# A unit of seven products for query block 4 and FFN block 12, and a new order of loads and transposes at the start

## The chip, the cores and the metric

The kernel runs on one core of one Trainium2 chip. The core has TensorE (PE in the profile: matmuls, with the loading of weights shown apart as PEld), VectorE (DVE), ScalarE (ACT), GpSimd (POOL), and SyncE (SP), which here only issues DMAs. The metric is the device time of one execution in microseconds; less is better.

## What is computed

A layer norm without weights, a linear attention of 32 heads and a gated feed-forward block share one normed input; the result is added to the input. There are 2048 tokens of width 640, and the inner width of the feed-forward block is 1728. All inputs are bf16.

```python
x  = A_x                                   # (1, 2048, 640)
xn = layernorm(x, eps=1e-5)
q, k, v = split(xn @ wqkv)                 # 32 heads of 20
phi = lambda t: where(t > 0, t + 1, exp(t)) + 1e-6
kv  = einsum("bhsd,bhse->bhde", phi(k), v);  z = phi(k).sum(tokens)
o   = (phi(q) @ kv) / (phi(q) . z + 1e-6)
s   = o @ wo
g   = silu(relu(xn @ w1) @ w2)             # w1 (640, 1728), w2 (1728, 640)
out = x + s * g
```

## The kernel before

**Tiles.** The tokens are 16 tiles of 128 (t = 0 to 15) and four chunks of 512 (j = 0 to 3). The width 640 is C = 5 pieces of 128. The inner width 1728 is 13 blocks of 128 (f = 0 to 12) and a half block of 64. A block of Q or of the feed-forward block for one chunk is five matmuls of 512 columns that add up in one bank of PSUM (`Q_mm` L764, `H_mm` L801); a tile of K is ten matmuls of 320 columns in two banks (`K_mm` L708). The half block is computed for two chunks at once by matmuls with 32 columns of weights, four beside each other (`H_half` L811).

**Units of seven.** Most blocks are made by a scheme with seven products instead of eight. `unit` (L1169) takes two blocks of weights and two chunks and forms the four results from seven products of two matmuls each, plus the fifth piece of the width: 18 matmuls, where four single blocks take 20. Its steps are named s1, s5, s6, s2, s7, s3, s4. The sums and differences of operands that it needs are made by DVE beforehand: `h_T` of the tokens (`T0` for chunks 0 and 1, `T1` for 2 and 3), `h_S`, `q_S`, `k_S` and `m_S` of the weights (`SH0` to `SH2`, `SQ`, `SK`, `SM`). In a unit ACT copies two products out (L1210), DVE adds in s6 (L1223), and DVE adds once more for the last result. `a` and `b` are units of the feed-forward block for chunks 0, 1 and for 2, 3, `p` and `q` those of Q, `k` of K. `m_unit` (L1287) pairs block 4 of Q with block 12 of the feed-forward block, since each is left over: before, `m1` does this for chunks 2 and 3 alone.

**The head.** While x and the weights come in, tiles 0 to 3 are not normed, but centred (`centre`, L671, with half the mean by DVE and half by ACT, or all by ACT), transposed by TensorE against an identity (`transposes`, L684), copied out of PSUM (`xcT_copy`, L691), and multiplied with the key weights (`K_mm`) and with five blocks of w1 (`HP`, L1365: 4, 5, 10, 11, 12). The scale 1/std is applied later: to K by ACT's exponential and relu (`K_evac`, L721), to the blocks of `HP` by DVE (`scale_h`, L1093, called by `ZS`). Means and variances come from DVE (`bn`, L633, two halves of a tile, and `aggr`, L638), the power -1/2 from POOL (L643). `LN_norm` (L653) writes the normed tile and issues its transposing DMA on SP (`xnT_dma`, L702), which gives the transposed tile `xnT` from which all the rest is computed. The first 32 matmuls of TensorE (`fill`, L602) compute nothing.

**Order.** All operations are recorded with what they read and write. `Sched.place` (L189) then plans every engine with estimated durations. TensorE and SP keep the order in which their operations are recorded; ACT, DVE and POOL do so up to `end_of_head` (L186), and behind it take the most urgent of the first 60 that can run. The recorded order is written by hand in the head (L576 to L592 the loads, L835 to L889 and L1377 to L1392 the rest), and behind it is the text `PROGRAM` (L345), whose words `play` (L1569) carries out: `p0.s1` is step s1 of unit p0, `H110` is block 10 of chunk 1, `Q14` is block 4 of Q in chunk 1, `Kb8` the second half of the key tile 8, `hh0` the half block of chunks 0 and 1, `n8` norm and transpose of tile 8, `xa` and `wa` loads of x and of w1. The text begins

```text
H110 H112 H14 H111 T0 H15 SQ SK xa Q14 a0.s1 a0.s5 Q04 a0.s6 p1.s5 p1.s1 ...
```

w1 comes in seven pieces, w1[0] to w1[6] (`w1_load`, L557; piece d holds the blocks 2d and 2d + 1, the last piece block 12 and the half block), the key weights in up to five (`wk_load`, L563). SP issues the loads of the head in this order: x0, key weights 0, 1, 2, 3-4, w1[2], w1[5], x4, x5, w1[6], x6, x7, w1[0], w1[3]; ACT issues x1, x2, x3. Then SP issues the transposes of tiles 4, 5, 6, 7, the loads of x8-9 and of wq, and the transposes of 0, 1, 2, 3.

**The end.** The last tile is finished in pieces (`s_last`, L1869): columns 0 to 160 and 160 to 320 (`LC`, L1649) come from the last ten matmuls, and each is multiplied, added to x and stored.

## Time and profile before

| | |
|---|---|
| time, median of 3 runs | 202.5 us (202.43 to 202.83) |
| span of the profiled execution, first to last instruction | 201.4 us |
| TensorE busy | 197.8 us (98%) |
| DVE, ACT, POOL busy | 175.1, 130.9, 37.9 us |
| granted TensorE clock | 1.000 |
| first matmul with data | 4.50 us |
| last matmuls begin, last instruction ends | 198.17 us, 201.4 us |

For the profiled execution the profile gives the span and no other time; the median of the runs is 1.1 us above it. In the profile, L714 is the line of the K matmuls, L804 of the blocks of the feed-forward block, L766 of Q, L1203 of the units of the first half, L1030 of the units behind them, L822 of the half blocks, L687 of the transposes, L975 the helper that records most of DVE's sums. A row of the timeline gives the start, the length, the engine and the line; neighbouring instructions of one kind are merged and counted. Matmuls are pipelined: the length of a single one holds the emptying of the pipe, so that the distance of two starts is what one costs. In the table of stages, the columns are the length, then the busy time of PE, PEld, DVE, ACT, POOL with counts, the granted clock, and DMA.

### The profile page before, as it was taken

The page shows a single profiled execution, that of the slowest core. Times are in us where ns is not written, and L with a number is a line of the kernel's source. Part 1 is how long each engine was busy: PE and PEld are TensorE (multiplying, and loading weights), DVE is VectorE, ACT ScalarE, POOL GpSimd, SP SyncE. Part 2 cuts the span into 40 slices and gives each one's busy share as a digit, 9 for nine tenths or more (in the row PEclk, how much of TensorE's full clock was granted, in tenths as well). Part 3 has the DMA queues.
Part 4 walks back from the last instruction along what each step waited for, and adds up shares of the span by engine and source line. Part 5 has one row for each costly group of instructions (what it writes and reads, how often), then busy time and mean ns, then how long its engine had stood idle before and what let it go on. Part 6 is the DMA issues. An engine that isn't in the chain of part 4 may idle for free.

```text
span 201.4 us, 3693 instructions
## 1 busy us (share of the span) xinstructions
PE 197.8 (98%) x1340; PEld 122.6 (61%) x1340; DVE 175.1 (87%) x413; ACT 130.9 (65%) x273; POOL 37.9 (19%) x66
## 2 busy tenths in 40 slices
PE   8999999999999999999999999999999999999995
PEld 7655644455455454445654777777777777767773
DVE  5988999999999888999975999999779786985674
ACT  6598957998999999978653224371555555445643
POOL 3174060363134654152200000000000000000000
PEclk9999999999999999999999999999999999999999
DMA  6977974765545896575910987865961244012103
GB/s 196 326 211 120 264 174 30 189 164 119 116 92 107 163 260 131 102 142 104 245 34 2 324 217 207 263 201 145 373 232 65 68 163 165 0 67 68 65 33 98
DMA packets 38471, 30.43 MB, mean 151 GB/s; under 512 B 13749, under 2 KB 38453, under 8 KB 38453
## 3 DMA queue, kind: packets, MB, share of 16 engines
q1 hardware_dynamic: 32581, 23.28, 41.2%
q0 software_dynamic: 4624, 5.57, 14.3%
q10 hardware_dynamic: 1248, 1.35, 2.1%
q8 instruction: 10, 0.16, 0.3%
q14 instruction: 8, 0.07, 0.1%
HBM read 15.81 MB, written 5.24 MB: 105 GB/s over the span
## 4 chain that ended last, share of the span: by engine, by line
PE 95%; DMA 3%; SPq 1%; DVE 0%; issue 0%; DVEq 0%
PE psT L1030 43%; PE psT L1203 31%; PE psT L714 8%; PE psT L804 5%; DMA reg<-in_A_wqkv_dram 3%; PE psT L1501 2%; PE psT L1835 1%; PE psT L822 1%; PE psT L766 1%; PE psT L1626 1%; PE psT L1600 1%; PE psT L934 1%; DVE reg L975 0%; SPq L564 0%; SPq L540 0%
## 5 line engine op out<-in xcount | busy, mean ns | idle before, releaser
L1203 PE MATMUL psT<-reg 128*128 128x512 bf16 (+2 forms) x159 | 41.7, 370 | 0.0
L1030 PE MATMUL psT<-reg,regH 128*128 128x320 bf16 (+1 forms) x224 | 34.8, 299 | 0.0
L1030 PE MATMUL psT<-reg 128*128 128x320 bf16 (+1 forms) x178 | 29.4, 299 | 0.0
L1030 PEld LDWEIGHTS psT<-reg,regH 128*128 128x128 bf16 (+1 forms) x224 | 21.8, 98 | 8.7 <-DVE psT L975 0.2
L1203 PEld LDWEIGHTS psT<-reg 128*128 128x128 bf16 (+1 forms) x159 | 15.5, 98 | 16.1 <-DVE reg L975 0.7
L902 POOL DMA_DIRECT2D regH<-reg x16 | 18.4, 1238 | 27.0 <-DMA regH<-reg 9.4
L1037 ACT ACTIVATE reg<-psT 128x320 f32<-128x320 f32 (+1 forms) x24 | 10.4, 435 | 17.4 <-PE psT L1030 15.9
L1030 PEld LDWEIGHTS psT<-reg 128*128 128x128 f16 (+1 forms) x178 | 17.3, 98 | 7.2 <-DVE regH L1256 0.4
L975 DVE TENSOR_TENSOR reg<-reg 128x1024 f16<-128x1024 bf16 (+10 forms) x30 | 18.9, 645 | 0.7 <-PE psT L1203 0.6
L1253 ACT ACTIVATE regH<-psT 128x512 bf16<-128x512 f32 (+1 forms) x24 | 14.6, 607 | 4.1 <-PE psT L1203 3.9
L975 DVE TENSOR_TENSOR psT<-psT,reg 128x320 f32<-128x320 f32 (+1 forms) x22 | 11.9, 542 | 5.6 <-PE psT L1030 5.1
L1030 PE MATMUL psT<-reg,pqT 128*128 128x320 bf16 (+1 forms) x84 | 16.3, 299 | 0.0
L1662 ACT ACTIVATE wv_sb<-psT 128x320 bf16<-128x320 f32 (+1 forms) x22 | 9.2, 423 | 10.3 <-PE psT L1030 9.9
L635 DVE BATCH_NORM_STATS2 stats<-reg 128x6 f32<-128x320 bf16 x32 | 13.9, 475 | 1.9 <-DMA reg<-in_A_x_dram 1.9
L1850 ACT ACTIVATE reg<-psT 128x640 bf16<-128x640 f32 (+1 forms) x14 | 8.0, 570 | 9.2 <-PE psT L1030 9.2
L714 PE MATMUL psT<-reg 128*128 128x320 bf16 x80 | 12.3, 299 | 0.0
L1037 ACT ACTIVATE psT<-psT 128x320 f32<-128x320 f32 x17 | 7.3, 427 | 6.8 <-PE psT L1030 6.8
L975 DVE TENSOR_TENSOR reg<-psT,reg 128x320 f32<-128x320 f32 (+2 forms) x19 | 9.5, 504 | 1.4 <-PE psT L1030 1.3
L781 ACT ACTIVATE regE<-psT 128x512 bf16<-128x512 f32 x16 | 9.6, 607 | 1.1 <-PE psT L766 0.5
L714 PEld LDWEIGHTS psT<-reg 128*128 128x128 bf16 x80 | 7.8, 98 | 4.3 <-ACT regH L808 0.3
L643 POOL TENSOR_TENSOR rsy<-rsv,mhalf 128x1 f32<-128x1 f32 x16 | 10.0, 622 | 1.3
L1030 PEld LDWEIGHTS psT<-reg,pqT 128*128 128x128 bf16 (+1 forms) x84 | 8.2, 98 | 3.2
(170 smaller groups left out, 397.9 us busy)
## 6 DMA issues: line engine op xcount, KB each, us to landing
regH<-reg POOLq DMA_DIRECT2D x16, 320.0 KB, 3.7
reg<-in_B_w_dram SPq DMA_DIRECT2D x12, 320.0 KB, 4.6
scr<-rden SPq DMA_DIRECT2D x4, 640.0 KB, 6.7
reg<-in_A_x_dram SPq DMA_DIRECT2D x4, 640.0 KB, 6.3
out_dram<-reg SPq DMA_DIRECT2D x14, 160.0 KB, 1.8
regE<-scr SPq DMA_DIRECT2D x3, 640.0 KB, 5.3
reg<-in_A_x_dram SPq DMA_DIRECT2D x4, 320.0 KB, 3.8
reg<-in_A_wo_dram SPq DMA_DIRECT2D x6, 160.0 KB, 5.0
```

The source lines that it names most:

```text
L635: sc.op("DVE", lambda eng: eng.bn_stats(stats[:, t, a, :], xv[:, HN * a:HN * (a + 1)]), R=[("xin", xs(t))], W=[("stats", t, a)])
L643: sc.op("POOL", lambda eng: eng.tensor_tensor(out=rsy[:, t:t + 1], in0=rsv[:, t:t + 1], in1=mhalf[:, :], op=ALU.pow), R=[("rsv", t), ("mha ...
L714: fns.append(lambda eng, a=a, k=k, lhs=lhs: eng.matmul(ps[bk[a]][:, 0:HN], lhsT=lhs, rhs=wk[:, k, HN * a:HN * (a + 1)], start=(k == 0), st ...
L781: exps.append(sc.op("ACT", lambda eng: eng.activation(out=e_, in_=src, func=ACTF.Exp), R=[key], W=[("er_e", es)]))
L804: sc.group("PE", [(lambda eng, k=k: eng.matmul(ps[b], lhsT=w1_col(k, P * f, P), rhs=src[:, k, :], start=(k == 0), stop=(k == C - 1))) for ...
L902: dma("POOL", lambda eng: eng.dma_start(zacc[a], src, **kw), R=[key] + after, W=[("zacc", a)], chain=zchain[a])
L975: sc.op("DVE", lambda eng: eng.tensor_tensor(out=out, in0=in0, in1=in1, op=op), R=R, W=W, extra=extra)
L1030: sc.group("PE", [(lambda eng, k=k, lhs=lhs, rhs=rhs: eng.matmul(ps[b][:, 0:HN], lhsT=lhs, rhs=rhs, start=(start and k == 0), stop=(k == n ...
L1037: sc.op("ACT", lambda eng: eng.activation(out=dst, in_=ps[b][:, 0:HN], func=ACTF.Copy), R=[("ps", b)], W=[dkey], extra=extra)
L1203: sc.group("PE", [(lambda eng, k=k, lhs=lhs, rhs=rhs: eng.matmul(ps[b][:, 0:nn], lhsT=lhs if tile is None else rhs, rhs=rhs if tile is Non ...
L1253: sc.op("ACT", lambda eng: eng.activation(out=dst, in_=ps[b], func=ACTF.Relu), R=[("ps", b)], W=[("hT", j, f)], extra=ex)
L1662: sc.op("ACT", lambda eng, lo=lo, hi=hi: eng.activation(out=g[:, lo:hi], in_=src[:, lo - HN * n:hi - HN * n], func=ACTF.Silu), R=[key, ("s ...
```

## The change

- The blocks H012 (in `HP`), H112, Q04 and Q14 go; the unit `m0` (block 4 of Q and block 12 of the feed-forward block, chunks 0 and 1) comes, behind `p1`. `SM`, its operand sums, moves ahead of it. `ZS` scales four blocks of chunk 0 instead of five.
- The head is now part of the text, ahead of a word `|`. Its key products are cut into smaller steps (`k012`: tile 0, pieces 1 up to 2).
- Loads of the head, all on SP but x1: x0, x2, key weights 0, 1, x3, key weights 2-3 (one transfer), x5, x4, key weight 4, x7, w1[2], x6, w1[5], w1[3], w1[0]. Then the transposes of tiles 5, 4, 2, 7, 6, 3, 0, 1 in one run, then wq, w1[6], x8-9, x12-13, x10-11, w1[4], the transpose of tile 8, and so on.
- The variance of tiles 1 and 2 comes from ACT (`square`: the sum of squares of the centred tile), not from DVE's statistics; their norm uses the mean that ACT had made.
- Behind the head four key tiles (5, 4, 7, 6), H15 and H111 stand ahead of the first unit; H110 and H14 stand between steps of units. `hh0` and `hh1` are no longer neighbours.
- `LC` is 0, 192, 320. The planner's estimates of loads change, and so may the order that it gives to ACT, DVE and POOL.

```diff
@@ Sched: estimates of DMAs
-            o.byt = 0.6 if o.turn else size / {"scr": 205e3}.get(names[0], {"scr": 240e3}.get(names[1], 310e3))
+            o.byt = 0.6 if o.turn else size / {"scr": 205e3}.get(names[0], {"scr": 240e3, "in_A_x_dram": 365e3, "in_A_wqkv_dram": 365e3}.get(names[1], 300e3))
...
+        lags = [(3.8, 0.6), (13.0, 0.7)]
...
-                line = max(est + (2.0 if c.turn else 1.5), line + (0.8 if turned and not c.turn else 0.0)) + c.byt
+                line = max(est + (2.0 if c.turn else 1.5), line + (turned != c.turn) * (0.4 if c.turn else 0.8)) + c.byt
+                if lags and line > lags[0][0]:
+                    line += lags.pop(0)[1]
@@ PROGRAM
-H110 H112 H14 H111 T0 H15 SQ SK xa Q14 a0.s1 a0.s5 Q04 a0.s6 p1.s5 p1.s1 n8 wa xb a0.s2 a0.s7 p1.s6 rb a0.s3 a0.s4 p1.s3 a1.s5 a1.s1 ...
+lx0 ba0 mh0 lx2 ax1 ma0 lk01 lk12 lx3 mv6 lk24 lx5 ce0 lx4 lk45 lx7 ma1 bb0 lw2 lx6 ma2 tr0 cd0 ce1
+lw5 pf3 cd1 lw3 ce2 k001 tr1 sq1 ma3 ag0 k012 cd2 tr2 ca5 cd3 ba3 cd4 mh3 ce3 k101 lw0 k112 k123 k201
+k134 S5 tr3 S4 k024 k045 sq2 ca7 ca6 N5 S7 N4 k145 k301 k312 N2 S6 ke0 bb3 k212 k223 k324 kr0 N7
+k235 ke1 kr1 k345 ag3 SH0_1 SH0_2 N6 P4 F1 N3 ke2 N0 kr2 P10 ke3 N1 lq P11 P5 lw6 F0 lx8 kr3
+|
+xb xa KT5 S8 wb n8 wa F2 n12 n11 KT4 SM F3 SK KT7 F4 KT6 xc rb H15 n10 F7 H111 SH0_3
+a0.s1 n9 n13 H110 n14 T0 F6 n15 SQ T1 a0.s5 a0.s6 H14 p1.s1 a0.s7 a0.s2 y1 p1.s5 a0.s4 y4 SH0_4 a0.s3 p1.s6 m0.s1
+p1.s2 m0.s5 m0.s6 m0.s2 p1.s3 m0.s7 p1.s7 m0.s3 m0.s4 p1.s4 Kb8 a1.s1 Ka8 a1.s5 p0.s5 a1.s6 p0.s1 Ka12 a1.s7 p0.s6 SH1 a1.s3 a1.s2 a1.s4
+a2.s5 hh0 a2.s1 p0.s2 p0.s7 Kb12 a2.s6 F5 Ka11 ...
+y6 k1.s6 k1.s2 y12 hh1 k1.s7 b0.s7 ...
@@ head
+    BY_ACT = (1, 2)
+    def square(t):
+        junk = ek[:, eks(t), 1, :]
+        sc.op("ACT", lambda eng: eng.activation(out=junk, in_=xn[:, t, :], func=ACTF.Square, scale=D ** -0.5,
+                                                accum_out=mv[:, t, 1:2]),
+              R=[("xn", t)] + ([("xn", t, 0)] if t == 0 else []), W=[("mv", t), ("ek_r", eks(t))])
+        root(t)
...
     def LN_norm(t):
+        mean, key = (msum[:, t, 1:2], ("msum", t, 1)) if t in BY_ACT else (mv[:, t, 0:1], ("mv", t))
@@ m_unit
-                sc.op("ACT", lambda eng: eng.activation(out=hT[:, NF - 1, schunk(j)], in_=ps[b], func=ACTF.Relu),
+                sc.op("ACT", lambda eng: eng.activation(out=(hT if j else hTh)[:, NF - 1, schunk(j)], in_=ps[b],
+                                                        func=ACTF.Relu), R=[("ps", b)], W=[("hT", j, NF - 1)])
@@
-    HP = (4, 5, 10, 11, 12)
+    HP = (4, 5, 10, 11)
@@
-    LC = [0, 160, 320]
+    LC = [0, 192, 320]
```

In the new head, `lx`, `ax`, `lk`, `lw` are loads (`ax` on ACT), `ba`, `bb`, `ag` statistics on DVE, `ma` a mean on ACT, `sq` the pass of `square`, `ce` centring, `tr` transposes on TensorE, `cd` and `ca` their copies on DVE and ACT, `ke` and `kr` the exponential and relu of K, `P` a block of `HP`, `KT` a whole key tile, `S` statistics, `N` norm with transposing DMA, `F` the end of a key tile on DVE, `pf` matmuls that compute nothing.

More of the change, by code (lines that the diff above doesn't have):

```diff
@@ L347 @@
+o3.s3 u5.s4 oS5 o3.s4 e3 oS4 o4.s1 u6.s1 uSa7 o4.s5 o4.s6 u6.s5 u6.s6 o4.s7 o4.s2 o4.s3 o4.s4 u6.s7 u6.s2 o5.s1 o5.s5 u6.s4 oS6 o5.s6
+u6.s3 o5.s7 u7.s1 o5.s2 o5.s3 u7.s5 uSb7 o5.s4 u7.s2 o6.s1 o6.s5 e0 o6.s2 o6.s6 f0 u7.s6 o6.s3 o6.s7 u7.s7 o6.s4 u7.s3 e1 f3 f1
+u7.s4 l0 l1
 """
```

183 lines of the change are left out of this document (88 added, 95 removed).

## The prediction

> **What bounds the kernel now.** I read the page first, then who waited for whom, then TensorE's instructions in order of time, then the loads.
>
> ```profile
> span 201.4 us, 3693 instructions
> PE 95%; DMA 3%; SPq 1%; DVE 0%; issue 0%; DVEq 0%
> ```
>
> ```profile
> PE psT L603 <- PEq L1946: 0.8, 1, 0.8
> PE psT L714 <- DMA reg<-in_A_wqkv_dram: 0.3, 1, 0.3
> ```
>
> The chain that ended last is TensorE for 95%, and in the whole run TensorE waits visibly twice: 0.8 us before its first instruction, and once for a piece of the key weights (wqkv). Everything else is either TensorE at work or the start and the tail. The start and one stretch behind it, from the timeline of TensorE:
>
> ```profile
> 4.50 0.63 PE L687 MATMUL psT<-ident,reg 128*128 128x128 bf16 x5
> 6.70 0.44 PE L687 MATMUL psT<-ident,reg 128*128 128x128 bf16 x5
> 7.43 1.53 PE L714 MATMUL psT<-reg,regX 128*128 128x320 bf16 x10 [0.29 <-DMA reg<-in_A_wqkv_dram]
> 12.07 5.56 PE L804 MATMUL psT<-regX,reg 128*128 128x512 bf16 x25
> 17.50 5.59 PE L714 MATMUL psT<-reg 128*128 128x320 bf16 x40
> 22.93 5.56 PE L804 MATMUL psT<-reg 128*128 128x512 bf16 x25
> 28.33 1.24 PE L766 MATMUL psT<-reg 128*128 128x512 bf16 x5
> 29.41 0.59 PE L1203 MATMUL psT<-reg 128*128 128x512 bf16 x2
> ```
>
> The first column is the start. 25 matmuls of 512 columns go from 22.93 to 28.33: 5.40 us, 0.216 each, 1.08 for a block of five. 40 of 320 columns go from 17.50 to 22.93: 0.136 each, 1.36 for a key tile. The two stretches follow each other without a gap. So from 7.43 on the time is the number of matmuls, and what the change can do is take matmuls away, or put waits between them; a faster DVE or ACT in itself is worth nothing.
>
> **Part 1: the unit of seven for query block 4 and FFN block 12.** It removes the head's `H_block(0, 12)`, H112, Q04 and Q14, each five matmuls of 512 columns: 20. The unit m0 has 2+3+3+3+2+2+2+1 = 18 (the dictionary in `unit`, L1187). Two fewer at 0.216: **-0.43 us**, all on TensorE. What hides the unit's evacuations is that ACT has room and DVE is paid for below.
>
> **Part 2: the two half blocks.** Before, `hh0 hh1` stand side by side in the program; after, `hh0` stands between `a2.s5` and `a2.s1`, and `hh1` between `y12` and `k1.s7`. These are matmuls of 32 columns of weights, four at a time:
>
> ```profile
> 51.77 0.38 PE L1203 MATMUL psT<-reg 128*128 128x512 bf16 x1
> 52.07 2.34 PE L822 MATMUL psT<-reg 128*32 128x512 bf16 x40
> 54.35 0.60 PE L1203 MATMUL psT<-regE,reg 128*128 128x512 f16 x2
> ```
>
> One matmul of 512 columns stands at 51.77 and the next instruction starts at 52.07: 0.30 instead of 0.216, so 0.08 to go in. The 40 are ten rounds, 10 x 0.216 = 2.16, and take 52.07 to 54.35, 2.28: 0.12 to come out. One stay costs 0.20 us; there will be two stays instead of one: **+0.20 us**. No semaphore is involved, so nothing hides it.
>
> **Part 3: the order of the loads in the head.** Before, SP issues x0, then the key weights in pieces k0, k1, k2, k3-4; ACT issues x1, x2, x3 beside it. After, SP issues x0, x2, k0, k1, x3, k2-3 (one transfer), x5, x4, k4, x7, ...; ACT issues only x1. Issue times and the time from issue to landing (last column) of the pieces that matter:
>
> ```profile
> 0.79 0.40 SPq L540 DMA_DIRECT2D reg<-in_A_x_dram  x1
> 1.25 1.85 SPq L564 DMA_DIRECT2D reg<-in_A_wqkv_dram  x4
> ```
>
> ```profile
> reg<-in_A_x_dram SPq DMA_DIRECT2D x1, 160.0 KB, 2.5
> reg<-in_A_x_dram ACTq DMA_DIRECT2D x1, 160.0 KB, 2.7
> reg<-in_A_wqkv_dram SPq DMA_DIRECT2D x1, 160.0 KB, 5.2
> reg<-in_A_wqkv_dram SPq DMA_DIRECT2D x1, 320.0 KB, 5.7
> ```
>
> ```profile
> 2.19 5.20 DMA reg<-in_A_wqkv_dram
> ```
>
> x0 lands at 0.79 + 2.5 = 3.3. k2, the third of the four wqkv pieces, is issued at 2.19 (chain) and lands at 7.38; with x0, x1, k0, x2, k1, x3 ahead of it, it is the 7th transfer of 160 KB. k3-4, the last of the four, issued 0.45 later, lands at about 2.65 + 5.7 = 8.35, as 8th and 9th: 0.48 each. In the new order k2 comes together with k3, as 7th and 8th (x0, x1, x2, k0, k1, x3 ahead): 7.38 + 0.48 = **7.86**.
>
> TensorE's work ahead of the first use of k2 is the same in both: three transposed tiles, and four pairs for k0 and k1 (`k001 k012 k101 k112` against `K_mm(0,2,0,1)`, `K_mm(0,2,1,KA)`, `K_mm(1,4,0,KA)`: 8 matmuls). The last of it, the third transposed tile, was over at 6.70 + 0.44 = 7.14, and the wait ended at 7.43. The new DVE order puts one `bn` of tile 0 ahead of the copies of the transposed tiles:
>
> ```profile
> L635 DVE BATCH_NORM_STATS2 stats<-reg 128x6 f32<-128x320 bf16 x32 | 13.9, 475 | 1.9 <-DMA reg<-in_A_x_dram 1.9
> ```
>
> That moves TensorE by 0 to 0.475, to 7.14 to 7.62, in any case before k2-3; the wait ends at 7.86 + 0.05 = 7.91. Against 7.43 that is **+0.47 us**. Bounds: if the transfers keep the pace of the first two, whose landings are 0.79 + 2.5 = 3.3 and 0.96 + 2.7 = 3.7, k2-3 would be there at 3.3 + 7 x 0.4 = 6.1, TensorE would go on at about 7.2, and the term is -0.23; if the pair lands when k3-4 did, 8.35, it is +0.97. I take the row that has the same bytes ahead.
>
> Behind it: k4 is 11th, 7.86 + 3 x 0.48 = 9.3; `k045` comes ten matmuls and one transposed tile (at most 0.44) later, 7.91 + 10 x 0.136 + 0.3 = about 9.55. Cover 0.25; if it is gone it costs what is missing. x5 lands 9th, 7.86 + 0.48 = 8.35, and x4 near 8.8.
>
> **Part 4: the transposing DMAs in one run.** SP's issues in the old order, the group of the wq load, and what a norm waits for:
>
> ```profile
> 20.34 0.47 SPq L545 DMA_DIRECT2D reg<-in_A_wqkv_dram  x1
> ```
>
> ```profile
> L703 SPq DMA_TRANSPOSE reg<-reg x8: 1200/1299/1809, 14.1 to 25.5; - x8
> ...
> DMA to landing us min/median/max: 2.6/3.0/5.4
> ```
>
> ```profile
> reg<-in_A_wqkv_dram SPq DMA_DIRECT2D x1, 800.0 KB, 5.3
> ```
>
> ```profile
> L639 DVE BATCH_NORM_AGGREGATE mv<-stats 128x2 f32<-128x12 f32 x16 | 3.3, 204 | 0.3
> ```
>
> ```profile
> L643 POOL TENSOR_TENSOR rsy<-rsv,mhalf 128x1 f32<-128x1 f32 x16 | 10.0, 622 | 1.3
> ```
>
> SP issues one each 1.3 us. New: the first tile (5) is normed about 10.5 (x5 at 8.35, two `bn` 0.95, an aggregation 0.2, POOL's power 0.62, the rest for the hand-overs and the norm), and w1[0] is issued by then, by the pace of the old one, whose 17 loads were out by 10; SP's eight issues then take until 10.5 + 8 x 1.3 = 21 at the earliest, and the last tile lands 2.6 to 3.0 later, 23.5 to 24. Queued behind them on SP are the wq load, w1[6] and x8. Who waits: the key tiles 5, 4, 7, 6 from 12.07 + 0.48 + 4 x 1.08 = 16.9 on (tile 5 must have landed, 10.5 + 3.0: covered), and `a0.s1`, which needs all eight tiles, at 16.9 + 4 x 1.36 + 2 x 1.08 (H15, H111) = **24.5**. Covered by 0.5 to 1 us; cost 0, and if the cover is gone, what is missing. One wait is added on DVE: in the head, `SH0_1` stands ahead of the norms 6, 3, 0, 1 and needs w1[0], the last load.
>
> ```profile
> 9.07 1.04 SPq L560 DMA_DIRECT2D reg<-in_B_w_dram  x2
> ```
>
> ```profile
> reg<-in_B_w_dram SPq DMA_DIRECT2D x2, 320.0 KB, 6.0
> ```
>
> The last two of the old order were issued at 9.07 and half a microsecond later and landed 6.0 later in the median, 15.1 to 15.6. New, with less ahead, w1[0] lands at 14 to 15.6, and norm 6 comes at 15 to 16.5, where its place in SP's run is 10.5 + 4 x 1.3 = 15.7. So the cover at `a0.s1` may shrink by 0.8, to nothing in the worst of this. The old kernel first used them at 29.41, so a late tile was free there and is not here. wq (800 KB) was issued at 20.34 and landed 5.3 later; new, issued at about 21.5, it lands near 26.5, and `p1.s1` needs it at 24.5 + 2 x 0.22 + 2 x 1.08 + 4 x 0.22 = 28.0. Cover 1.5.
>
> **Part 5: variance of tiles 1 and 2 on ACT, tail.** Four `bn` and two aggregations leave DVE; ACT takes two `Square` passes of 640 columns, beside TensorE's wait for k2-3, and their results go to the norms of tiles 1 and 2, which are 3rd and 8th in the run. A pass of that width:
>
> ```profile
> 3.79 0.72 ACT L666 ACTIVATE regE<-reg 128x640 bf16<-128x640 bf16 x1
> ```
>
> Cost 0; what it costs without that cover is that ACT's copy of a transposed tile behind a pass comes 0.72 later. The last block is cut 192 + 128 instead of 160 + 160: the last product and sum on DVE are 32 columns shorter.
>
> ```profile
> 198.79 0.67 DVE L975 TENSOR_TENSOR reg<-psT,wv_sb 128x160 bf16<-128x160 f32 x2 [0.22 <-PE psT L1835]
> 199.37 0.38 DVE L975 TENSOR_TENSOR reg<-reg 128x160 bf16<-128x160 bf16 x2
> ```
>
> Two of 160 take 0.67 and 0.38, so 32 columns of one product and one sum are 0.2 x (0.33 + 0.19) = 0.10, but the piece before, which is ahead of them on DVE, grows by the same: between -0.10 and 0; I take **-0.03**, since the rows stand close behind each other.
>
> **Sum.** -0.43 + 0.20 + 0.47 - 0.03 = +0.21. The span goes from 201.4 to 201.6. The median of the runs is 202.5, 1.1 above the profiled span; I keep that distance: **202.7 us**. A difference under 0.2%, 0.4 us, can't be told from none.
>
> **Rivals.**
>
> B, the weights are not late. The wait at 7.43 was the only one behind the start; if the transfers come at the early pace, the term of part 3 is -0.23 instead of +0.47: 202.0 us. For it: the first landings are 0.4 apart. Against it: the following ones in the same trace were not.
>
> C, slower: DVE becomes the pace of the middle. It decides if DVE, and not TensorE, is late at the first operands of a unit.
>
> ```profile
> 25.00:30.00 5.00, 5.00 (x25) 2.25 (x23) 4.97 (x13) 2.78 (x5) 3.26 (x9) 1.00 0.85 182
> 40.00:60.00 20.00, 20.00 (x135) 10.08 (x134) 19.95 (x54) 19.07 (x41) 8.09 (x14) 1.00 0.55 120
> ```
>
> The first figure is the length, then come PE, its weight loads, and DVE: 4.97 of 5, 19.95 of 20. It has no room in these stretches.
>
> ```profile
> L975 DVE TENSOR_TENSOR psT<-psT,wv_sb 128x512 f32<-128x512 f32 x10 | 6.9, 694 | 1.0 <-PE psT L1203 1.0
> L975 DVE TENSOR_TENSOR regH<-psT,wv_sb 128x512 bf16<-128x512 f32 x8 | 5.5, 687 | 1.2 <-PE psT L1203 1.1
> L1266 DVE TENSOR_SCALAR regH<-regH 128x512 bf16<-128x512 bf16 x10 | 3.0, 322 | 0.1
> ```
>
> m0 adds a sum for `s6` (0.69), one for the last product (0.69) and its maximum (0.32): 1.70. The head gives back 4 x 0.475 + 2 x 0.204 = 2.31. Against C: on balance DVE has 0.6 less. For it: the 1.70 falls where DVE is full, units start at 24.5 instead of 29.4, and the four sums of `SM` come earlier too. Price between 0 and 1.7; half of that, 0.8, gives 203.5 us.
>
> D, `Square` needs another table on ACT.
>
> ```profile
> 0.80 1.28 ACT L573 ACT_TABLE_LOAD   x1 [0.80 <-PEq L1946]
> ```
>
> One load serves Copy, Relu and Exp here, for 1.28 us. If Square had another set there would be one load ahead of it and one ahead of the next Exp, 2.56 us on ACT, of which the copies of tile 3 and the first exponentials hide all but about 0.7: 203.4 us. For and against it the trace has nothing but that one load covered three functions. The Trainium skill, "ScalarE: Activation LUTs", section "Table sets: the hidden batching unit", says that cheap functions stand in every set; its list does not name Square. By that D falls away, and no run here shows it yet.
>
> **How the numbers follow.** A, the sum: 0.40. B: 0.28. C: 0.27. D: 0.05. The range takes in B below with 0.1 to spare and C to just above its middle: 201.9 to 203.6. Faster (below 202.1): most of B, 0.25. Slower (above 202.9): C, D and the upper end of A, where k2-3 is later than 7.9 or k4 misses: 0.37. Same: the rest, 0.38.
>
> **What would show it.** Right: TensorE's wait for wqkv grows from 0.3 to about 0.7, the second stretch of K starts near 7.9, two separate rows of L822 x20, matmuls of L804 and L766 gone or fewer, and no new row in TensorE's waits. Wrong: K going on at 7.2 (B); rows of TensorE waiting for DVE between 24 and 68 (C); a second and third table load before 12 us (D); TensorE waiting for transposed tiles at 24.5, which part 4 denies.

## The result and the profile after

The changed kernel takes **203.76 us** in the median of 8 runs (203.15 to 205.34), the kernel before 202.65 (8 runs beside them, 202.40 to 203.35): ratio 1.0058, 95% interval 1.0035 to 1.0082. It is slower by 0.6%, 1.1 us above the old time and 1.06 above the forecast. Its profiled execution took 203.75, span 202.5.

The head of the page and of the chain of waits, then who TensorE waited for (in all, times, longest):

```profile
span 202.5 us, 3683 instructions
PE 82%; DMA 10%; DVE 6%; issue 1%; SPq 0%; DVEq 0%
```

```profile
PE psT L605 <- PEq L1967: 0.8, 1, 0.8
PE psT L1629 <- DVE reg L936: 0.5, 1, 0.5
PE psT L991 <- DVE reg L936: 0.2, 1, 0.2
```

Before, the chain was TensorE for 95%. Now 10% of it are DMAs and 6% VectorE (DVE), and there are two rows in which TensorE waits for sums of DVE; the wait for wqkv has gone from this list. TensorE in order of time, at the places where it stood still or which the prediction named:

```profile
5.70 0.69 PE L733 MATMUL psT<-reg,regX 128*128 128x320 bf16 x2
...
7.19 1.52 PE L733 MATMUL psT<-reg,regX 128*128 128x320 bf16 x10
...
12.36 0.81 PE L823 MATMUL psT<-regX,reg 128*128 128x512 bf16 x3
...
24.27 0.59 PE L1164 MATMUL psT<-reg 128*128 128x512 bf16 x2
...
45.83 1.26 PE L841 MATMUL psT<-reg 128*32 128x512 bf16 x20
47.02 0.39 PE L1164 MATMUL psT<-reg 128*128 128x512 bf16 x1
...
57.69 1.26 PE L841 MATMUL psT<-reg 128*32 128x512 bf16 x20
58.89 0.31 PE L1164 MATMUL psT<-regH,reg 128*128 128x320 f16 x1
...
125.79 0.45 PE L1629 MATMUL psT<-reg 128*128 128x320 bf16 x2 [0.45 <-DVE reg L936]
...
136.05 0.72 PE L991 MATMUL psT<-reg 128*128 128x320 f16 x4
...
182.18 0.58 PE L991 MATMUL psT<-reg,pqT 128*128 128x320 f16 x3 [0.18 <-DVE reg L936]
```

For the whole run I take, for each matmul, the time from its start to the next start, less what an undisturbed one takes (0.216 for 512 columns, 0.136 for 320, the prediction's rows). What is left are gaps, mostly waits. The span is then: start and gaps up to 12.5 us, gaps from 12.5 to 105, gaps behind 105, the matmuls themselves, and the tail behind the last matmul. The two kernels were profiled again later (`before_again`, `after_again`, `after_3`). In some traces ten records of matmuls are missing; each leaves a hole of 0.216, which is counted as a matmul.

| profile | start, gaps to 12.5 | 12.5 to 105 | behind 105 | matmuls | tail | span |
|---|---|---|---|---|---|---|
| before | 5.35 | 0.37 | 0.24 | 192.83 | 2.62 | 201.4 |
| before_again | 5.18 | 0.33 | 0.24 | 192.83 | 2.62 | 201.2 |
| after | 5.65 | 0.44 | 1.44 | 192.42 | 2.56 | 202.5 |
| after_again | 5.91 | 0.46 | 0.98 | 192.42 | 2.56 | 202.3 |
| after_3 | 5.70 | 0.53 | 1.31 | 192.42 | 2.57 | 202.5 |
| mean difference | +0.49 | +0.13 | **+1.00** | -0.41 | -0.06 | +1.1 |

Four of the five columns are close to the prediction (the start in part by luck, as part 3 below says). The third was not in it: TensorE stands still behind 105 us, in the first profile by 0.61 at 125.79, 0.23 at 136.05 and 0.35 at 182.18. The chain of waits (start, length, what), followed back from 136.05:

```profile
108.48 0.37 SPq L1059
108.84 0.04 issue
108.89 5.20 DMA reg<-in_B_w_dram
114.09 0.04 DVEq L330
...
117.53 0.61 DVE regE L899
118.14 0.02 issue
118.16 1.76 DVE rden L908 x2
...
121.97 5.00 DMA scr<-rden
126.96 0.02 issue
126.98 6.77 DMA reg<-scr
133.75 0.02 issue
133.78 1.57 DVE pqT L929 x2
135.35 0.02 issue
135.37 0.64 DVE reg L936
136.00 0.05 issue
136.05 40.38 PE psT L991 x296
```

DVE waits for a piece of w2 until 114.09; behind that in its fixed order stand the eviction of the denominators (L899) and four reciprocals (L908); these are stored, loaded again in another layout, and divide the queries (L929). In the kernel before the same steps, and the first sum of 2240 columns behind them, were, in DVE's order of time,

```profile
110.83 0.69 DVE L938 TENSOR_SCALAR regE<-psT 128x512 f32<-128x512 f32 x1 [0.16 <-PE psT L934]
111.56 0.95 DVE L947 RECIPROCAL rden<-regE 128x128 bf16<-128x128 f32 x1
...
116.97 1.31 DVE L975 TENSOR_TENSOR reg<-reg 128x2240 f16<-128x2240 bf16 x1
```

The eviction is 6.6 us sooner there, and the first divide started at 127.77 instead of 133.78. But the chain shows only what released each step last, and the divide is not late by the reciprocals alone. DVE in the changed kernel, in order of time, at its waits for the two DMAs of the chain:

```profile
114.17 1.32 DVE L936 TENSOR_TENSOR reg<-reg 128x2240 f16<-128x2240 bf16 x1 [1.73 <-DMA reg<-in_B_w_dram]
...
132.90 0.62 DVE L936 TENSOR_TENSOR regE<-regH,regE 128x896 f16<-128x896 bf16 x1 [2.17 <-PE psT L991]
133.78 1.56 DVE L929 TENSOR_TENSOR pqT<-pqT,reg 128x1536 bf16<-128x1536 bf16 x2 [0.25 <-DMA reg<-scr]
```

Ahead of the divide stands a sum that waits 2.17 for TensorE; the reciprocals delay the divide by 0.25. The sum at 114.17 waits 1.73 for w2; in the kernel before, the first sum of that form starts at 116.97, behind the reciprocals and without a wait, and the last piece of w2 had landed at 115.28. The word `dn`, TensorE's matmuls for these denominators, stands later in the new text: in the old one ahead of `g0.s3`, in the new one behind `g0.s7`. The change rewrote the second half of the text too, and that half is what this document's diff leaves out.

### The profile page after: what moved, and what is told of

Same layout as the page of the kernel before. It is cut to its first block, busy times and chain, and to the rows that moved or that the text cites. A ratio compares the mean times of both kernels' runs of the same rounds, so it can differ in the third digit from the quotient of the medians.

```text
span 202.5 us, 3683 instructions
## 1 busy us (share of the span) xinstructions
PE 198.5 (98%) x1338; PEld 122.4 (60%) x1338; DVE 173.0 (85%) x409; ACT 131.9 (65%) x278; POOL 37.1 (18%) x66
## 3 DMA queue, kind: packets, MB, share of 16 engines
q0 software_dynamic: 4624, 5.57, 14.1%
## 4 chain that ended last, share of the span: by engine, by line
PE 82%; DMA 10%; DVE 6%; issue 1%; SPq 0%; DVEq 0%
PE psT L1164 33%; PE psT L991 31%; PE psT L733 8%; PE psT L823 4%; DMA reg<-scr 3%; DMA reg<-in_B_w_dram 3%; DMA scr<-rden 2%; PE psT L1494 2%; DVE reg L936 2%; DVE rden L908 2%; PE psT L1838 1%; DMA reg<-in_A_x_dram 1%; PE psT L841 1%; DVE pqT L929 1%; DVE psT L936 0%
## 5 line engine op out<-in xcount | busy, mean ns | idle before, releaser
L1164 PE MATMUL psT<-reg 128*128 128x512 bf16 (+2 forms) x166 | 43.3, 370 | 0.0
L991 PE MATMUL psT<-reg 128*128 128x320 bf16 (+1 forms) x178 | 29.4, 299 | 0.1
L936 DVE TENSOR_TENSOR reg<-reg 128x1024 f16<-128x1024 bf16 (+11 forms) x30 | 18.9, 644 | 2.9 <-DMA reg<-in_B_w_dram 1.7
L1665 ACT ACTIVATE wv_sb<-psT 128x320 bf16<-128x320 f32 (+2 forms) x23 | 9.7, 424 | 9.6 <-PE psT L991 8.6
L936 DVE TENSOR_TENSOR psT<-psT,reg 128x320 f32<-128x320 f32 (+1 forms) x21 | 11.3, 540 | 3.4 <-PE psT L991 3.4
L637 DVE BATCH_NORM_STATS2 stats<-reg 128x6 f32<-128x320 bf16 x28 | 12.2, 475 | 1.2 <-DMA reg<-in_A_x_dram 1.2
L936 DVE TENSOR_TENSOR psT<-psT,wv_sb 128x512 f32<-128x512 f32 (+1 forms) x14 | 9.1, 651 | 2.8 <-PE psT L1164 1.4
L1171 ACT ACTIVATE psT<-psT 128x512 f32<-128x512 f32 (+1 forms) x18 | 10.6, 593 | 0.7 <-PE psT L1164 0.6
```

The lines of the kernel that those rows point to most:

```text
L637: sc.op("DVE", lambda eng: eng.bn_stats(stats[:, t, a, :], xv[:, HN * a:HN * (a + 1)]), R=[("xin", xs(t))], W=[("stats", t, a)])
L936: sc.op("DVE", lambda eng: eng.tensor_tensor(out=out, in0=in0, in1=in1, op=op), R=R, W=W, extra=extra)
L991: sc.group("PE", [(lambda eng, k=k, lhs=lhs, rhs=rhs: eng.matmul(ps[b][:, 0:HN], lhsT=lhs, rhs=rhs, start=(start and k == 0), stop=(k == n ...
L1164: sc.group("PE", [(lambda eng, k=k, lhs=lhs, rhs=rhs: eng.matmul(ps[b][:, 0:nn], lhsT=lhs if tile is None else rhs, rhs=rhs if tile is Non ...
L1171: sc.op("ACT", lambda eng: eng.activation(out=dst[:, 0:nn], in_=ps[b][:, 0:nn], func=ACTF.Copy), R=[("ps", b)], W=[dkey], extra=extra)
L1665: sc.op("ACT", lambda eng, lo=lo, hi=hi: eng.activation(out=g[:, lo:hi], in_=src[:, lo - HN * n:hi - HN * n], func=ACTF.Silu), R=[key, ("s ...
```

## Experiments

**Theory 1:** the new order of the second half (all words behind `a3.s4`) makes the gaps behind 105 us. **Theory 2:** the changed first half leaves DVE or the DMA queues late, and the second half only shows it. A narrower form of theory 1: it is `dn` alone. Beside them the prediction's own terms were tried one by one. In `old_back`, `dn_early`, `k0_first` and `hh_side` line numbers are one higher. All profiles in the columns of the table above (4.45 in `late_old` holds 1.7 that is no wait, see there):

| profile | start, gaps to 12.5 | 12.5 to 105 | behind 105 | span | median us | ratio to before |
|---|---|---|---|---|---|---|
| old_back | 5.96 | 1.07 | 0.24 | 202.3 | 203.60 | 1.0041 to 1.0066 |
| old_back_2 | 6.25 | 0.93 | 0.24 | 202.4 | 203.70 | 1.0030 to 1.0061 |
| mid_old | 5.85 | 0.71 | 0.93 | 202.5 | 204.00 | 1.0055 to 1.0116 |
| late_old | 5.75 | 0.67 | 4.45 | 205.9 | 207.27 | 1.0158 to 1.0237 |
| end_old | 6.10 | 0.57 | 1.68 | 203.3 | 204.81 | 1.0084 to 1.0120 |
| new_back | 5.34 | 2.76 | 1.12 | 204.7 | 205.99 | 1.0142 to 1.0218 |
| dn_early | 6.08 | 1.25 | 2.50 | 204.8 | 206.05 | 1.0148 to 1.0192 |
| dn_do | 5.49 | 1.47 | 0.99 | 202.9 | 204.38 | 1.0078 to 1.0135 |
| dn_pin | 5.58 | 0.85 | 2.40 | 203.8 | 205.26 | 1.0119 to 1.0156 |
| dn_pin_k | 5.69 | 0.77 | 2.41 | 203.8 | 205.73 | 1.0141 to 1.0184 |
| k0_first | 5.80 | 2.11 | 1.18 | 204.0 | 205.33 | 1.0126 to 1.0160 |
| k2_alone | 5.66 | 1.13 | 0.93 | 202.7 | 203.91 | 1.0052 to 1.0076 |
| hh_side | 6.29 | 1.35 | 1.11 | 203.7 | 204.89 | 1.0098 to 1.0132 |
| hh_pin | 5.68 | 1.75 | 2.49 | 204.9 | 205.09 | 1.0108 to 1.0145 |
| best | 5.50 | 3.37 | 0.24 | 204.1 | 205.53 | 1.0124 to 1.0159 |

### The second half in the old order: old_back

```diff
-... q1.s1 a3.s4 b2.s5 GT1 y10 q1.s6 q1.s2 b2.s1 Ka15 ...
+... q1.s1 a3.s4 q1.s6 b2.s5 q1.s2 b2.s1 Ka15 q1.s7 w2a ...
```

> The changed kernel with the words of its text from just behind a3.s4 on put in the order of the kernel before; the first part of the text is untouched. Theory 1 (the new order of the second half makes the three late waits of TensorE): the waits for DVE at 125.8, 136.05 and 182.2 us go, 0.61 + 0.23 + 0.35 = 1.19 us, and the profiled span falls from 202.5 to 201.3, about 1.2 us under the changed kernel's median, near the kernel before or 0.1 under it. Theory 2 (the changed first half leaves DVE or the DMA queues late, and the second half only shows it): the waits stay, the span stays at 202.3 to 202.7. The waits before 8 us stay by both.

Measured: the three late waits are gone, 0.24 behind 105 us, as in the kernel before. TensorE's waits in `old_back`:

```profile
PE psT L734 <- DMA reg<-in_A_wqkv_dram: 1.2, 1, 1.2
PE psT L606 <- PEq L1968: 0.8, 1, 0.8
```

But the time is 203.60, hardly below the changed kernel. What was won behind 105 us is lost in front of it: 1.32 at 8.05 waiting for wqkv, 0.27 at 24.84, 0.26 at 79.31. Theory 1 holds for the late gaps; for the time it was not decided by this run.

### The same again, and the second half cut in two: after_3, old_back_2, mid_old, late_old

Two more profiles of the unchanged kernels belong here:

> The changed kernel once more, unchanged, so that its start can be read a second time. If where the early transfers are held up differs from run to run: k2-3 lands near 7.9 as in old_back and dn_early (7.91, 8.04) and not at 7.29, the waits for wqkv ahead of the first K stretch sum to 0.9 to 1.5 and not 0.40, and the span is 202.9 to 203.3. If it belongs to the kernel: the landings of the first profile come again within 0.15 us, span 202.4 to 202.6. The waits at 125.8, 136.05 and 182.2 come again by both, 1.0 to 1.3 us together.

> The kernel before once more, one profile, to see how far its start differs from run to run. If only the changed kernel's start is uneven: k2 lands at 7.3 to 7.5 again, the first block of matmuls of 512 (L804) starts at 12.0 to 12.2, span 201.3 to 201.5. If both are uneven: k2 lands anywhere from 7.0 to 8.0 and the block starts up to 0.5 later or sooner.

`after_again`: 203.69 us (ratio 1.0043 to 1.0074), k2-3 at 7.88, the waits ahead of K 1.2 together; behind 105 us 0.98, without the wait at 125.8. `before_again`: k2 at 6.99, first block of 512 columns at 11.9, span 201.2. So the start differs from run to run in both kernels.

> The changed kernel a third time, beside the three below. Gaps of TensorE behind 105 us of 0.9 to 1.5, as in its first two profiles (1.44, 0.98), the wait of 0.35 near 182 among them; the first block of 512-column matmuls starts at 12.3 to 12.7; median 203.5 to 203.9.

> old_back a second time, in the same call as the changed kernel. The order of all engines up to the words behind a3.s4 is that of the changed kernel to the last instruction, so what differs ahead of it is chance. If the second half alone makes the loss and the start of old_back's first profile was chance: gaps behind 105 us of 0.25 again, and a median 0.5 to 1.1 under after_3's. If what is won behind 105 us is lost again in front in each run: gaps of 0.25 behind 105 us and a median within 0.3 of after_3's, with the same waits at 8.0, 24.8 and 79.3 in the profile.

```diff
 mid_old:  -... a3.s4 b2.s5 GT1 y10 ... dn do0 ... W2 u0.s3 W0 (new order) u1.s1 ...
           +... a3.s4 q1.s6 b2.s5 ... dn g0.s3 ... W1 W3 W0 (old order) u1.s1 ...
 late_old: only the words behind W0 in the old order
```

> The changed kernel with the words from behind a3.s4 up to W0 in the old order (the b and g units, the w2 loads, dn, the transposes uT, the kv and W blocks) and those from there on (u and o units) as changed. If the waits at 125.8 and 136 belong to dn and what stands around it: they go, the one of 0.35 at 182 stays; gaps behind 105 us of 0.5 to 0.7. If they belong to the order of the u steps: they stay.

> The changed kernel with only the words behind W0 in the old order (u and o units, the later divides). If the wait at 182 belongs to the order of the u and o steps: it goes, the waits at 125.8 and 136 stay; gaps behind 105 us of 0.5 to 1.1. If it is VectorE's backlog from dn's lateness: it stays, 0.3 or more behind 150 us, as it did in end_old, which moved only the words behind o3.s4 and had 1.26.

`after_3` is 203.73 us (1.0028 to 1.0061) and `old_back_2` 203.70. Again 1.31 against 0.24 behind 105, and again the same time: `old_back_2` loses 0.55 more in the start and 0.40 more between 12.5 and 105. Of that, the gap of 0.26 at 79.3 to 79.5 is in both `old_back` runs and, at 78.9, in `mid_old`, and in no kernel with the new text there: it belongs to the old words at the seam behind `a3.s4`. The rest lies where no engine's order differs from the changed kernel's.

`mid_old` has neither the waits at 125.8 and 136 nor the one at 182.2, although the last part of its text is the new one, but 0.33 at 134.1 and 0.36 at 139.2. `late_old` tells most. DVE, then TensorE:

```profile
133.47 1.56 DVE L929 TENSOR_TENSOR pqT<-pqT,reg 128x1536 bf16<-128x1536 bf16 x2 [2.55 <-DMA reg<-scr]
```

```profile
136.16 1.22 PE L991 MATMUL psT<-reg 128*128 128x320 f16 x7 [2.34 <-DVE reg L936]
```

With the old order of the u and o units behind the new `dn`, DVE stands for 2.55 us in front of the divide until the reciprocals are there, at 133.47, and TensorE loses 2.51. The rest of its 4.45 is mostly no wait: behind that stall, from 137.06 to 140.47, the granted clock is half (0.63 in the mean from 136 to 140, 1.00 there in every other profile), a matmul of 320 columns takes 0.267 instead of 0.136, and that costs 1.7. So the late reciprocals are real, and the new order of the u steps is fitted to them: it hides the 2.51 at this place down to 0.18 to 0.35. The two parts belong together, and of the orders tried only both in the old order have no gap.

### The mirror image, and the end alone: new_back, end_old

```diff
 new_back (kernel before): words behind a3.s4 in the changed kernel's order
 end_old  (changed kernel): words behind o3.s4 in the old order
-... e3 oS4 o4.s1 u6.s1 uSa7 o4.s5 o4.s6 u6.s5 u6.s6 o4.s7 o4.s2 o4.s3 o4.s4 u6.s7 ...
+... oS4 o4.s1 o4.s5 o4.s2 o4.s6 u6.s1 u6.s5 u6.s6 o4.s3 o4.s7 u6.s7 o4.s4 ...
```

> The kernel before with the words of its text from behind a3.s4 on put in the order of the changed kernel; its own first half, its own units, its own planner's costs. The mirror image of old_back. Theory 1 (the order of the second half makes the late waits): TensorE waits for VectorE at 125 to 138 us, 0.3 to 0.9 together, and 0.35 near 181, which the kernel before does not have, and the time is 0.7 to 1.2 above the kernel before. Theory 2 (they come from what the changed first half leaves late): no wait over 0.15 behind 105 us, time within 0.3 of the kernel before.

> The changed kernel with only the words behind o3.s4 (the last units o4 to o6, u6, u7) in the order of the kernel before. The wait of 0.35 at 182.2, which all eight kernels so far with the changed text there have (0.344 to 0.363), is put down to o4.s7, o4.s2, o4.s3, o4.s4 standing in a row without a step of u6 between them. If so: that wait goes, the waits at 125 to 136 stay, the time is 0.35 under the changed kernel. If it comes from VectorE's backlog further ahead: it stays or moves, same time.

`new_back` is slower than the kernel before by 1.8%, more than expected: 0.66 at 138.3 and 0.21 at 176.2 are of the expected kind, but 2.40 at 101.8 is new (TensorE in order of time):

```profile
101.82 0.40 PE L921 MATMUL psT<-const-bfloat16-1.0,regE 128*128 128x1 bf16 x10 [2.23 <-DVE regE L975]
```

The late gaps come with the new second half here too, 1.12 against 0.24; beside them the seam costs more with the old first half, so that the run does not show 1.0 as the price of the second half by itself. In `end_old` the wait stays, 0.38 at 182.32, and three more come at 173.8 to 177.6. That the steps of o4 in a row make it is refuted; it was there, 0.34 to 0.38, in all changed kernels with the new words around W0, and went when either the words up to W0 (`mid_old`) or those behind it (`late_old`) were old. It is no backlog of DVE: in the changed kernel DVE stands idle for 1.36 until 181.24, then does two sums of TensorE's results, and the operand that TensorE waits for comes third, at 182.04. What makes it stays open.

### dn alone: dn_early, dn_do, dn_pin

```diff
 dn_early:
-... g0.s5 b4.s3 g0.s6 g1.s1 ... g0.s7 dn do0 ...
+... g0.s5 b4.s3 dn g0.s6 g1.s1 ... g0.s7 do0 ...
 dn_do, as dn_early and:
-... uT3 do1 g0.s4 uSa0 wv1 uSb0 rc0 g0.s2 ...
+... uT3 g0.s4 uSa0 wv1 uSb0 rc0 do1 g0.s2 ...
```

> The changed kernel with one word moved: dn, the matmuls of the denominators with their eviction, stands right behind b4.s3 and not behind g0.s7. Theory 1a (the chain denominator, reciprocal, store, load, divide starts 5 us later than before, since DVE waits for the w2 load ahead of the denominator's eviction, and DVE's fixed order stands behind it): the eviction is on DVE before 112 us, the first store of the reciprocals is issued near 117 and not 122, the divide of DVE starts near 128 and not 133.8, and TensorE's waits of 0.61 at 125.8 and 0.23 at 136.05 go: span 201.7, 0.8 us under the changed kernel. The wait of 0.35 at 182.2 stays. Theory 1b (the w2 load that DVE waits for until 114.1 us makes the two waits, wherever dn stands): both stay, the span stays within 0.2 of 202.5.

> dn_early with one more word moved: do1, the second store of the reciprocals, stands behind the second load of the wv weights and the first load of reciprocals (rc0), as in the kernel before. dn_early had its two waits of TensorE gone and a new one of 1.79 at 126.7, for a wv load that was issued at 119.3 behind two stores (117.3, 118.0) and landed at 126.6. If that load lies behind the stores in the DMA queues: it now lands 3 to 4 us sooner, the wait goes, TensorE has less than 0.2 us of waits between 105 and 150 us, and the time is 1.8 to 2.1 under dn_early's and 0.6 to 0.9 under the changed kernel's of this call. If the load is late for another reason: a wait of 1 us or more stays at 126 to 127.

In `dn_early` the eviction is at 110.93 and the store at 117.29, as theory 1 had it, and the waits at 125.8 and 136 are gone. In their place TensorE waits 1.79 at 126.67. SP, ACT's queue, then TensorE:

```profile
117.29 1.34 SPq L916 DMA_DIRECT2D scr<-rden  x2
```

```profile
119.31 0.38 ACTq L568 DMA_DIRECT2D wv_sb<-in_A_wqkv_dram  x1
```

```profile
126.67 0.53 PE L1604 MATMUL psT<-reg,wv_sb 128*128 128x120 bf16 x7 [1.63 <-issue]
```

The piece of the value weights that L1604 reads was issued behind two stores of 640 KB and landed 7.3 us later, at 126.6. `dn_do` moves the second store behind it: TensorE is at those matmuls at 124.5 without a wait, and the median falls from 206.05 to 204.38, though the other engines' orders and the start differ too. The gap is gone, as expected; but one of 0.33 at 129.0 is new (an addition on DVE behind the divide), the one at 182 stays, and behind 105 us it has 0.99, no less than `after_again`. That `dn`'s place alone makes the loss is not borne out.

The planner (L182) chooses the orders of DVE, ACT and POOL from the text, so a word moved changes them elsewhere too. `dn_pin` therefore has the text of `dn_do`, but writes the orders of the changed kernel down and moves in them only the eviction and two reciprocals.

> The changed kernel with dn behind b4.s3 on TensorE, do1 behind rc0 on the DMA queue, and on VectorE only the eviction of the denominators and the first two reciprocals (0.69 + 0.95 + 0.9 = 2.5 us) moved ahead of uT3, into the 2.4 us in which VectorE now waits for the w2 load; every other order of ScalarE, VectorE and GpSimd is held. If that wait with the denominators behind it makes the loss: the divides start at 128 to 130 and not 133.6 to 133.8, TensorE's waits at 125.8 and 136 go, gaps behind 105 us fall from 0.98 to 1.44 (three profiles) to 0.5 to 0.7, the wait near 182 staying, and the time is 0.4 to 0.9 under 203.7. If VectorE has no room in that stretch anyway: waits of 0.4 or more somewhere between 110 and 140 us, time within 0.3 of 203.7.

DVE in `dn_pin`, in order of time:

```profile
114.47 1.32 DVE L936 TENSOR_TENSOR reg<-reg 128x2240 f16<-128x2240 bf16 x1 [0.40 <-PE psT L991]
115.71 0.49 DVE L936 TENSOR_TENSOR psT<-psT,reg 128x320 f32<-128x320 f32 x1
116.11 0.68 DVE L899 TENSOR_SCALAR regE<-psT 128x512 f32<-128x512 f32 x1
```

The three pieces did not come into the idle stretch: it lies ahead of `uT1`, not of `uT3`, and they went in behind `uT1`. The eviction is at 116.11 instead of 117.44, and the divide at 133.74, as in the changed kernel. Yet the waits at 125.8 and 136 are gone; there are others, 0.52 at 120.2, 0.53 at 143.3, 0.69 at 145.9. DVE's two waits for DMAs are gone as well: 0.40 for TensorE ahead of the sum at 114.47 in place of 1.73 for w2, and none for the reciprocals at the divide, which stands at the same time since the sum ahead of it still waits 2.17 for TensorE.

Side by side, the profiles with the new order there tie each of the two waits to one of DVE's. TensorE's wait at 125.8 is DVE's wait for w2 less 1.12: 1.73, 1.66, 1.25 and 1.31 give 0.61, 0.54, 0.13 and 0.20 (`after`, `after_3`, `k2_alone`, `hh_side`), 1.14, 1.12 and 1.03 give none (`after_again`, `k0_first`, `end_old`), and 2.57 in `hh_pin` gives 1.13 with 0.31 shortly ahead of it. The wait at 136 is the divide's wait for the reciprocals less 0.02: 0.25, 0.37, 0.20 and 0.21 give 0.23, 0.35, 0.18 and 0.19 (`after`, `after_again`, `after_3`, `k2_alone`); in `late_old` 2.55 gives 2.51. So the first wait comes from the sum on w2, which stands in DVE's order ahead of the landing of w2, and the second from the late reciprocals.

### The terms of the start: k0_first, k2_alone, dn_pin_k

```diff
 k0_first:
-lx0 ba0 mh0 lx2 ax1 ma0 lk01 lk12 lx3 ...
+lx0 ba0 mh0 lk01 ax1 ma0 lx2 lk12 lx3 ...
 k2_alone (orders held):
-... mv6 lk24 lx5 ...
+... mv6 lk23 lk34 lx5 ...
 dn_pin_k: dn_pin with
+lx0 ba0 mh0 lk01 ax1 ma0 lx2 lk12 lx3 mv6 lk23 lk35 ce0 lx5 lx4 lx7 ...
```

> The changed kernel with the first wqkv load (k0) issued ahead of the x2 load. If the loss at the start is the place of k0 behind x2 among the first transfers: k0 lands at about 5.2 or sooner and not 5.57, the wait of TensorE for wqkv at 5.70 (0.40) shrinks or goes, the first K stretch starts at 5.2 to 5.3, and up to 0.4 us are won, if x2, now later by one transfer (0.4 to 0.5), does not make the transposes of tile 2 wait in its place: span 202.1 to 202.3. If some DMA engines stand still between 4.2 and 6.5 us whatever is queued, k0 lands after 5.4 all the same: span 202.4 to 202.6.

> The changed kernel with k2 and k3 as two loads one behind the other instead of one load of both, as the kernel before has k2 alone; the order of ScalarE, VectorE and GpSimd is held as in the changed kernel. The prediction's third term: the first K matmuls on k2 need only k2, which now lands one transfer (0.43) sooner, so TensorE's waits for wqkv shrink by 0.3 to 0.45 against the changed kernel of this call, and the time by as much. If the hold-up of the early transfers ends at a fixed time and k2 lands in it either way: within 0.1 of the changed kernel.

> dn_pin with the first loads in the order of the kernel before: k0 ahead of x2, k2 alone, k3 with k4 behind it, x5 and x4 one transfer later; the other orders held as in dn_pin. If the weights are what the start loses by: k2 lands at 6.8 to 7.4 and not 7.3 to 8.2, the first block of 512-column matmuls starts at 12.0 to 12.2 and not 12.2 to 13.0, 0.4 to 0.6 under dn_pin in front. If the transposed tiles then are the bound: a wait at a0.s1 (24.3 to 24.8) takes up what was won, and the time is within 0.2 of dn_pin.

`k0_first`: k0 lands at 4.01, and x2 at 5.18 and k1 at 6.13 instead; 0.23, 0.32 and 0.54 are waited for in place of the one wait, and the start is 5.80, no gain. `k2_alone`: k2 lands at 7.36, k3 at 7.76; the wait is now for k0 (0.74 at 5.74); start 5.66, 0.25 less than `after_again`, and 0.51 lost at 24.78, at `a0.s1`. `dn_pin_k`: k2 at 7.16, and no gain over `dn_pin` (5.69 against 5.58). With the weights sooner, TensorE waits for other things: in `dn_pin_k` 0.40 at 6.32 for k1, and 0.24 at 6.85 for the third tile, whose load x2 now lands at 5.52 (4.07 in the changed kernel). From who TensorE waited for in `dn_pin_k`; the first row, the transposes behind DVE's centring of the first tile (L699), is in `after_again` and `after_3` too, with 0.49 and 0.34:

```profile
PE psT L706 <- DVE reg L699: 0.3, 1, 0.3
PE psT L733 <- DMA reg<-in_A_wqkv_dram: 0.2, 1, 0.2
```

What the start wins is also cut off further on: in `k2_alone` the last transposed tile landed at 24.69 and `a0.s1` started 0.09 behind it.

### The two half blocks: hh_side, hh_pin

```diff
-... a2.s5 hh0 a2.s1 ... y12 hh1 k1.s7 ...
+... a2.s5 a2.s1 ... y12 hh0 hh1 k1.s7 ...
```

> The changed kernel with hh0 moved down to its neighbour hh1, so that TensorE enters the 32-column mode once and not twice for them. The prediction's second term: 0.20 us less (two stays of 0.19 to 0.20 besides the matmuls become one), span 202.3. If the stays cost nothing by themselves: no change, 202.5. If the four half matmuls are wanted sooner by DVE or ScalarE than hh1 stands: a new wait behind 47 us.

> The changed kernel with hh0 next to hh1 as in hh_side, but with the order of ScalarE, VectorE and GpSimd held as in the changed kernel (only ScalarE's two evictions of hh0 move with it). The second term: one stay in the 32-column mode less, 0.20 us less than the changed kernel in TensorE's own accounting of gaps, three stays become two. If the waits that hh_side had for VectorE and ScalarE between 46 and 65 us (0.9 together) come from the place of hh0 itself, they are here too; if they came from the order that the planner chose anew, they are gone.

One stay in the 32-column mode is gone in both, and both are slower. With the orders held, `hh_pin` has 0.46 at 46.6, 0.25 at 53.7 and 0.21 at 55.9; the first, in TensorE's order of time:

```profile
46.61 1.25 PE L1164 MATMUL psT<-reg 128*128 128x512 bf16 x5 [0.30 <-ACT regH L1214]
```

So the waits come from the place of `hh0` itself: its 20 matmuls keep TensorE busy where ACT's eviction is not ready. The second stay cost 0.20 and bought more. The profile of `hh_pin` is that of its slowest run (206.16, median 205.09), so its row is some 1 us above what the median has.

### Three repairs at once: best

```diff
 loads as in dn_pin_k, the second half as in old_back, and
-... H111 SH0_3 a0.s1 n9 n13 H110 n14 ...
+... H111 SH0_3 H110 a0.s1 n9 n13 n14 ...
```

> Three edits of the changed kernel at once, each for one measured loss: the wqkv loads in the order of the kernel before (k0 ahead of x2, k2 alone, k3 and k4 behind it), H110 ahead of a0.s1 as cover for the transposing DMAs, and the second half in the old order (old_back). If the losses are what they were read to be: the first block of matmuls of 512 starts at 12.0 to 12.3, a0.s1 has no wait, there is no wait over 0.15 behind 105 us, and the time is that of the kernel before less 0.43 (two matmuls) plus 0.20 (one stay) plus 0 to 0.3: 202.3 to 202.6. If each edit moves its wait to a new place, as dn_early's did: 203.0 or more.

205.53 us. No gap behind 105 us but the usual 0.24, for the third time with the old second half; no wait at `a0.s1`; but 0.55 at 26.2, 0.25 at 26.9, 0.59 at 29.4 and more up to 58, for DVE by the profile. TensorE in order of time:

```profile
26.20 0.60 PE L1164 MATMUL psT<-regE,pqT 128*128 128x512 f16 x2 [0.39 <-DVE regE L936]
...
29.42 0.61 PE L1164 MATMUL psT<-regX,reg 128*128 128x512 f16 x2 [0.43 <-DVE psT L936]
```

H110 is no longer behind the first step of a0, where it gave DVE time for the next operands, and the last transposed tile landed at 24.77 (24.08 in the changed kernel); which of the two weighs more was not tried. No version beats the kernel before.

## Why the prediction was wrong

- **Part 1, two matmuls fewer:** -0.43 forecast, -0.41 in the sum of the matmuls (328 of 512 columns instead of 330, and the cut of the last block). Right.
- **Part 2, the second stay:** +0.20 forecast. In the rows of L841, 20 matmuls are 5 rounds, 1.08, and take 45.83 to 47.02 and 57.69 to 58.89, 1.19 and 1.20; with what it costs to go in, each stay is 0.2. Between 12.5 and 105 us the changed kernel has 0.13 more gaps. Right.
- **Part 3, the loads:** the size came out right, in part by luck, and the reason half. The first profile spoke against it: k2-3 landed at 7.29, TensorE waited 0.40 at 5.70 for k0 and not for k2. That was one draw: over 13 profiles with this load order k2-3 landed at 7.29 to 8.24, 7.80 in the mean (forecast 7.86), and the start cost 5.87 against 5.29 in the three with the old start, +0.58 (forecast +0.47). The luck is in the row that the sum started from: k2 landed at 7.38 there, but at 6.99 and 6.82 in the other two profiles of the old start, so in the mean the pair lands 0.74 later and not 0.48. With the weights sooner (5.50 to 5.80 in `best`, `k2_alone`, `dn_pin_k`, `k0_first`) only a third or so comes back, and that is less than the 13 differ among themselves (5.49 to 6.29).
- **Part 4, the transposing DMAs:** the last tile landed at 24.08 (forecast 23.5 to 24) and `a0.s1` started at 24.27, in none of the three profiles of the changed kernel after a wait. But the cover of 0.5 to 1 us was put too high: it is 0.07 to 0.10. In ten of the other profiles TensorE lost 0.14 to 0.51 here, starting 0.09 behind the last landing (24.36 to 25.00). This part was right for this kernel by a tenth of a microsecond, which is luck.
- **Part 5 and rival D:** the tail is 0.06 shorter (forecast 0.03). The trace has two table loads, at the start and at 98.60, ahead of the first Silu, none by Square:

```profile
L595 ACT ACT_TABLE_LOAD x1 | 1.3, 1283 | 0.8 <-PEq L1967 0.8
L1906 ACT ACT_TABLE_LOAD x1 | 1.3, 1283 | 0.0
```

 The Trainium skill, "ScalarE: Activation LUTs", section "Table sets: the hidden batching unit", has cheap functions in every set and does not name Square among them; here no load came for Square either. Rival B's sign, K going on at 7.2, is in the first profile (7.19), but not its price: TensorE had waited for k0 before, and the start was 0.30 longer, not shorter. Rival C named the right kind of cause, TensorE waiting for DVE, and its price, 203.5, was near by luck; its place, 24 to 68 us, has no such wait in the changed kernel.
- **The step that failed** is the sentence behind the timeline of the start: "from 7.43 on the time is the number of matmuls, and what the change can do is take matmuls away, or put waits between them". It is true, and then waits were looked for only up to 68 us. The change reorders most of the words behind `a3.s4` too: `dn`, the w2 loads, the stores of the reciprocals, the u and o steps. No part worked that out, so the term was silently 0; it measured **+1.00** (0.98 to 1.44 of gaps against 0.24). The sum with it is 202.7 + 1.0 = 203.7; measured 203.76. That these gaps come with the new order is shown (0.24 in three kernels with the old one). For two of the three waits the reason is shown too: 0.61 of the first profile is DVE's wait for w2 less the 1.12 that was covered, 0.23 its wait for the reciprocals less 0.02. The one of 0.35 near 182 is open, and no single word makes them all: moving single words moved the waits.

What also stays open: with the old second half put back, the time did not fall, because the gaps ahead of 105 us were larger in those profiles (7.03 and 7.18 against 6.09 to 6.37, start included), and only 0.26 of that could be tied to the text. Chance at the start is not enough to explain it: the medians of 5 and 12 runs are 203.60 and 203.70, where 203.73 less 1.0 and plus 0.26 would be 203.0. So it is shown where the changed kernel's 1.1 us lie, but not that the old order behind `a3.s4` gives them back.

## What to carry to other kernels

When a change rewrites an order written by hand, compare all of it, and for each chain that leaves the engine (evict, store, load, divide) note when it starts in the old and the new order; a diff that is too long to read is no reason to price it at 0. Here, where the bounding engine hardly waits, the order was one piece: its parts are fitted to each other, and putting back one part of the second half cost 0.1 to 1.7% more (the last in part by the clock). The chain that ended last names what released each step, not what each step cost: at the divide the chain shows a DMA of 6.77 us, and the wait for it was 0.25. And a start that depends on the first DMAs is read from several profiles: two landing times of the same load differed by 0.5 us and more here, in both kernels.

## What was not expected of the hardware

- The first transfers of one kernel land at quite different times from run to run: k2-3, always issued at 3.13 to 3.15, landed at 7.29 to 8.24. In most profiles the transfers of 160 KB land about 0.4 apart up to about 4 us; then one or two land 1 to 2 us behind the one before, now k0 (4.18 first, 5.57 last of its 16 parts in the changed kernel), now k1 (4.44 and 6.54 in `old_back_2`).
- A load of 320 KB issued on another engine's queue right behind two stores of 640 KB landed 7.3 us after its issue (`dn_early`) and 3.2 us when issued ahead of them (117.56 to 120.73 in the changed kernel).
- The reload of the reciprocals took 6.77 us in the changed kernel, issued at 126.98 beside a store that landed at 130.22, against 4.81 (122.01 to 126.82) in the kernel before. There two stores were issued 0.4 and 1.0 behind it and landed later, so what makes the difference is not shown.
- In `late_old` a stall of TensorE of 2.51 us was followed, 0.9 us after its end, by 3.41 us at half the granted clock; behind the stall of 2.40 in the profile of `new_back` the clock stayed at 1.000, but two of its six runs have a mean of 0.992, as `late_old` has.
